# Eight plain chunks and twenty product groups instead of twelve and twelve, with attention spread into the groups

## The chip, the cores and the metric

One core of one Trainium2 chip runs the whole computation in one launch. The metric is device microseconds of one execution, as a median of several. A profile of one further execution shows what each engine did: TensorE (PE; its weight loads are PEld), VectorE (DVE), ScalarE (ACT), GpSimd (POOL), and SyncE (SP), which here only issues DMAs.

## The reference

For x of 2048 tokens by 576 features, in fp32, two branches are added to x:

```
xn  = layernorm(x)
A   = attention(xn @ wqkv) @ wo        # 32 heads of 18; each token sees 8 tokens: itself and 2, 4, ... 14 back
h   = gelu(xn @ w1), its four quarters shifted by +1, -1, +2, -2 tokens
x1  = x + h @ w2
B   = x1 + gelu(layernorm(x1) @ w3) @ w4   # w3: 576 x 4608, w4: 4608 x 576
out = x + A + B
```

## The kernel before

**Precision.** All products are taken in a split form: each fp32 operand is written as a high part, which is its cast for TensorE, and a low part, the rest. ScalarE makes the high part, VectorE subtracts it for the low part (`split_w`, `split_ws`, `split_op`, `low_part`). A product of two operands then takes three matmuls.

**Stages in order.** The qkv projection writes q, k and v to a DRAM buffer `qkvd`. The token mixer gives x1 in `Y` (16 tiles of 128 tokens) and its layernorm, transposed, in DRAM (`xn`) and on chip (`x1n`). Then comes the wide MLP, which the change is about, and at the end the product of the attention result with `wo`.

**The wide MLP.** The 4608 hidden features are 36 slices of 128, taken in pairs. The first `NPL` = 12 pairs are *plain chunks*: for each chunk and each of four blocks of 512 tokens (a *unit*, 48 in all) two `up` products give the hidden values, a gelu follows, and four `down` tiles of 128 tokens add hidden @ w4 to the result. The downs of a unit are run after the ups of the next one. The other `NWP` = 6 pairs are done by a seven-product scheme on 2 x 2 blocks (two halves of the features, two blocks of 512 tokens, two slices): a *group* `q` forms seven products P1 to P7 of seven matmuls each from sums and differences of the operands, and runs the eight down tiles D0 to D7 of the group before. A pair takes two groups, one for each half `sb` of the tokens, so there are 12 groups. The sums of x1n are made in DRAM (`sums`), loaded by `get_op` and split by `split_op` (keys B11, B21, B22, T1 to T4); those of w3 are loaded by `load_pair`, formed by `combine` on VectorE and split by `split_a` and `split_s`.

**The order around the change.** Everything is emitted by hand, and each engine runs its list in that order. In a group the string `ORDER` (or an entry of `ORDERS`) gives the sequence of P's and D's on TensorE, and `at(item, f)` puts further work behind an item in the lists of the other engines. Four PSUM buffers of one bank serve the products; P1, P6, P7 and P4 accumulate onto one of them, and before each of P6, P7 and P4 ScalarE must have copied the state (`keep`, L1063). VectorE's `z_add` (L1066) adds the other products. Two PSUM buffers serve the downs in turn.

**Evicting a down tile.** For the six tiles not in `YD` VectorE adds PSUM to `Y` (L827). For the ten in `YD` ScalarE copies PSUM to a staging tile (L823) and GpSimd issues a DMA that adds it to DRAM (`yd`, L824). In the plain stage the staging is three of the `YD` slots of `Y` (9, 11, 10), in the groups a pool `evp` of five tiles. Other `YD` slots hold scratch: the raw w4 of `load_w4`, and Z1 to Z4.

**Attention in the background.** `attention` is a generator that emits VectorE operations for eight sets of four heads, and yields an estimate of the time of each. `bg(us)` adds to a debt and emits operations while the debt is positive. In plain units from u = 4 on the debt grows by `RATE[0]` = 9.0 us a unit. `yield None` marks the point before the exp on ScalarE; the generator goes on from it only in a call with `late` true. What is left three units before the end of the plain stage is emitted at once. Before a group reads attention's result, `load_o` loads it from DRAM (`od`), and `o_turn` transposes it on VectorE; this begins in the group with `z == -5`, group 7 before and group 15 after.

Of the kernel before, what the change touches and what calls it, by code (L numbers as in the profile page):

```python
# [8 lines left out]
F32 = mybir.dt.float32  # L9
# [8 lines left out]
NT = S // 128  # L18
# [18 lines left out]
NPL = 12  # L37
# [20 lines left out]
def fused_block(ctx, tc, x, wqkv, wo, w1, w2, w3, w4, out):  # L58
# [42 lines left out]
    bncnt = [0]  # L101
    ztail = {}
# [455 lines left out]
    def split_w4(c, step=None):  # L558
        t = W4["pair", c]
        raw = Y[:, 0:4, :].rearrange("p (a b) c -> p a b c", b=2)[:, :, 1, :]  # L560
        if step != 1:
            act.copy(t[:, :, 0, :], raw)  # L562
        if step != 0:
            dve.tensor_tensor(t[:, :, 1, :], raw, t[:, :, 0, :].bitcast(F32), op=ALU.subtract)  # L564
# [107 lines left out]
    def attention(ap):  # L672
        mask = ap.tile([128, TPP, W], F32, name="mask")
        pool.memset(mask, 0.0)
        for w in range(1, W):
            pool.memset(mask[0:1, 0:DIL * w, w:w + 1], -1e9)
# [14 lines left out]
        def av(g):  # L691
# [8 lines left out]
            o = ap.tile([128, TPP * GH, HD], F32, name="o")  # L700
            for w in range(W):
                r0 = halo - DIL * w
                vv = v[:, r0:r0 + TPP, :].rearrange("p j (h d) -> p (j h) d", d=HD)
                dst = o if w == 0 else ap.tile([128, TPP * GH, HD], F32, name="prod")
# [6 lines left out]
            sp.dma_start(od.rearrange("(p j) d -> p j d", p=128)[:, :, g * GC:(g + 1) * GC],  # L711
                         o.rearrange("p (j h) d -> p j (h d)", h=GH))
# [5 lines left out]
        for g in range(NG + 1):  # L718
            if g < NG:
# [3 lines left out]
                for w in range(W):  # L723
                    prod = ap.tile([128, TPP * GH, HD], F32, name="prod")
                    r0 = halo - DIL * w
                    dve.tensor_tensor(prod.rearrange("p (j h) d -> p j (h d)", h=GH), q,  # L726
                                      k[:, r0:r0 + TPP, :], op=ALU.mult)
                    yield 1.3
                    dve.tensor_reduce(Lf[:, :, w], prod, axis=AX.X, op=ALU.add)  # L729
                    yield 1.3  # L730
# [62 lines left out]
    def low_part(h, g):  # L793
        dve.tensor_tensor(h[:, 1, :], g, h[:, 0, :].bitcast(F32), op=ALU.subtract)  # L794
# [12 lines left out]
    def down(t, parts, pd):  # L807
# [17 lines left out]
        else:  # L825
            yv = Y[:, t, :].rearrange("p (h c) -> p h c", h=2)
# [44 lines left out]
    def split_op(sb, k):  # L871
        xt = area[sb][k]
# [16 lines left out]
    def load_pair(q):  # L889
        c0 = 2 * (NPL + pair(q)) * 128  # L890
        odd = (q - (q > NWP)) % 2
        st = WS["st", q] = (evp if odd else wspool).tile([128, 3, 4, 128], F32, name="w3st")
# [4 lines left out]
        for a in range(0, 96, 32):  # L897
# [3 lines left out]
    def combine(q):  # L901
        st = WS["st", q]
        for o, i, op in ((1, 0, ALU.subtract), (0, 2, ALU.add), (2, 1, ALU.subtract),
                         (3, 2, ALU.subtract)):
            dve.tensor_tensor(st[:, 1:3, o, :], st[:, 1:3, o, :], st[:, 1:3, i, :], op=op)
            dve.tensor_tensor(st[0:96, 0, o, :], st[0:96, 0, o, :], st[0:96, 0, i, :], op=op)


    def split_ws(dst, src, steps):
# [4 lines left out]
        if 2 in steps:  # L914
            dve.tensor_tensor(dst[:, 1:3], src[:, 1:3], dst[:, 3:5].bitcast(F32), op=ALU.subtract)
# [22 lines left out]
    RATE = [9.0, 2.0]  # L938
# [6 lines left out]
    for u, (c, b) in enumerate(units):  # L945
# [8 lines left out]
        for i in range(C):  # L954
# [18 lines left out]
            if z == -1:  # L973
                split_op(0, ("T2", "T1")[i])
        if u == 1:
            raw = x1n[3].bitcast(F32)
            pool.tensor_tensor(RS[2][:, 0, 0:1], raw[:, 4, 0:1], raw[:, 8, 0:1], op=ALU.mult)
        for j, (t, parts) in enumerate(prev):
            bg(r, j == 1)
# [8 lines left out]
            for f in {(-3, 1): (lambda: split_a(0),), (-3, 3): (lambda: combine(0),),  # L988
                      (-2, 1): (lambda: split_op(0, "T3"),), (-2, 3): (lambda: split_op(0, "T4"),),
                      (-1, 0): (lambda: split_s(0, (0, 1)),), (-1, 1): (lambda: split_s(0, (2,)),),  # L990
                      (-1, 3): (lambda: split_op(0, "B22"), lambda: split_a(1))}.get((z, j), ()):
# [13 lines left out]
        if z == -3:  # L1005
            while not state["done"]:
                bg(1e9)
            apc.__exit__(None, None, None)


            opc = tc.tile_pool(name="op", bufs=1, reuse_waits="tile")
            opool = opc.__enter__()
            evc_pool = tc.tile_pool(name="evp", bufs=1, reuse_waits="tile")
# [340 lines left out]
```

## Time and profile before

| | |
|---|---|
| median of 3 runs | 1289.2 us (1289.15 to 1290.45) |
| profiled execution | 1290.47 us, its span 1288.7 us |
| TensorE busy | 1272.9 us, 99% of the span |
| VectorE busy | 920.9 us, 71% |
| ScalarE busy | 558.3 us, 43% |
| granted TensorE clock | 0.999 |
| plain units | from 313 to 925 us of the span |
| product groups | from 925 to about 1211 us |

Matmuls are pipelined, so their durations overlap, and a time per matmul is best read as the distance of two starts. Shares of the other engines are means over stages with different loads. Where a row shows idle time, it is that of the engine just before the row, with what ended it.

### The profile page before, as it was taken

The numbers are of one execution on the slowest core, as the hardware profiler recorded it, in microseconds if no ns is written. First come the engines' busy times: TensorE is split into PE (matmuls) and PEld (weight loads), VectorE is DVE, ScalarE is ACT, GpSimd is POOL, SyncE is SP. The second block draws the span as 40 slices with busy tenths as digits, with TensorE's granted clock in tenths as the row PEclk, the third lists the DMA queues.
The fourth block names the chain that finished last, engine by engine and source line by source line (L and its number), as shares of the span: only waits on it lengthen the run. The fifth ranks groups of instructions, "written<-read, shape, count | busy, mean of one in ns | idle before, by whom it ended". The sixth has DMA issues, their size and how long they took to land. (4 is left out here: it accounts for less than half of the span.)

```text
span 1288.7 us, 19585 instructions
## 1 busy us (share of the span) xinstructions
PE 1272.9 (99%) x7594; PEld 1169.8 (91%) x7594; DVE 920.9 (71%) x1307; ACT 558.3 (43%) x900; POOL 214.2 (17%) x318
## 2 busy tenths in 40 slices
PE   9999999999999999999999999999999999999998
PEld 8999998899898989899999999988898898999998
DVE  6455534677568899999999999966766656676541
ACT  3322126516634434343434343433856567455530
POOL 2011100021221211221212121112111112112200
PEclk9999999999999999999999999999999999999999
DMA  7646874246896887987876877558847777788972
GB/s 209 158 115 138 171 176 142 75 123 182 197 269 146 166 165 195 193 167 150 176 155 145 184 134 158 90 113 188 193 80 137 150 167 163 169 209 180 265 251 83
DMA packets 196172, 210.21 MB, mean 163 GB/s; under 512 B 77920, under 2 KB 134176, under 8 KB 195952
## 3 DMA queue, kind: packets, MB, share of 16 engines
q1 hardware_dynamic: 165536, 144.82, 38.9%
q0 software_dynamic: 30544, 64.16, 32.2%
q8 instruction: 59, 0.97, 0.3%
q14 instruction: 33, 0.27, 0.1%
HBM read 112.98 MB, written 107.28 MB: 171 GB/s over the span
## 5 line engine op out<-in xcount | busy, mean ns | idle before, releaser
L819 PEld LDWEIGHTS ps<-w,c 128*128 128x128 f32 x3456 | 466.7, 188 | 14.3 <-DVE Y L827 4.2
L819 PE MATMUL ps<-w,c 128*128 128x288 f32 x3456 | 473.3, 294 | 5.3 <-DVE Y L827 2.9
L824 POOL DMA_DIRECT2D yd<-Y x125 | 109.2, 876 | 445.8 <-ACT Y L823 413.2
L823 ACT COPY Y<-ps 128x576 f32<-128x576 f32 x125 | 79.9, 640 | 162.6 <-PE ps L819 84.4
L794 DVE TENSOR_TENSOR c<-Y,c 128x512 fp32r<-128x512 f32 x144 | 98.9, 687 | 59.2 <-ACT Y L784 50.5
L783 ACT ACTIVATE c<-p 128x512 fp32r<-128x512 f32 x96 | 57.6, 600 | 191.9 <-PE p L800 191.9
L212 PE MATMUL ps<-WQ,xt 128*128 128x432 f32 x672 | 134.8, 360 | 0.0
L212 PEld LDWEIGHTS ps<-WQ,xt 128*128 128x128 f32 x672 | 125.6, 188 | 5.7
L726 DVE TENSOR_TENSOR prod<-q,k 128x1152 f32<-128x1152 f32 x64 | 86.6, 1353 | 10.4 <-DMA k<-qkvd 9.7
L827 DVE TENSOR_TENSOR Y<-ps,Y 128x576 f32<-128x576 f32 x108 | 81.2, 752 | 16.0 <-PE ps L819 15.8
L729 DVE TENSOR_REDUCE L<-prod 128x64 f32<-128x1152 f32 x64 | 86.5, 1351 | 1.1
L824 POOL DMA_DIRECT2D yd<-ev x55 | 47.8, 887 | 217.6 <-ACT ev L823 214.2
L800 PE MATMUL p<-xt,w3a 128*128 128x512 f32 x336 | 78.9, 391 | 1.5 <-ACT Y L784 1.5
L800 PE MATMUL p<-x1n,w3a 128*128 128x512 f32 x336 | 78.6, 390 | 0.0
L800 PE MATMUL p<-xt,w3s 128*128 128x512 f32 x336 | 78.5, 390 | 0.0
L800 PE MATMUL p<-x1n,w3s 128*128 128x512 f32 x336 | 78.5, 390 | 0.0
L705 DVE TENSOR_TENSOR prod<-v,L 128x1152 f32<-128x1152 f32 x56 | 75.8, 1353 | 0.8
L709 DVE TENSOR_TENSOR o<-o,prod 128x1152 f32<-128x1152 f32 x56 | 75.8, 1353 | 0.6
L800 PEld LDWEIGHTS p<-xt,w3a 128*128 128x128 f32 x336 | 62.2, 188 | 15.0 <-ACT Y L784 2.3
L119 POOL TENSOR_TENSOR rs<-rs,mhalf 128x1 f32<-128x1 f32 x48 | 30.9, 645 | 261.0 <-DVE rs L118 148.0
L800 PEld LDWEIGHTS p<-x1n,w3a 128*128 128x128 f32 x336 | 62.4, 188 | 12.6
L800 PEld LDWEIGHTS p<-xt,w3s 128*128 128x128 f32 x336 | 62.4, 188 | 12.6
(196 smaller groups left out, 1759.3 us busy)
## 6 DMA issues: line engine op xcount, KB each, us to landing
yd<-Y POOLq DMA_DIRECT2D x127, 288.0 KB, 5.4
yd<-ev POOLq DMA_DIRECT2D x55, 288.0 KB, 5.1
Y<-in_B_w_dram SPq DMA_DIRECT2D x23, 576.0 KB, 6.8
w3st<-in_B_w_dram SPq DMA_DIRECT2D x44, 256.0 KB, 6.1
qkvd<-stg SPq DMA_DIRECT2D x24, 432.0 KB, 3.5
xd<-st SPq DMA_DIRECT2D x16, 320.0 KB, 6.1
xd<-big SPq DMA_DIRECT2D x16, 320.0 KB, 7.8
xin<-in_A_x_dram SPq DMA_DIRECT2D x16, 288.0 KB, 3.8
```

Of the source, the lines that this page charges most:

```text
L212: pe.matmul(ps[:, h, :n], xs(a), ws(b, h), start=i == 0, stop=i == len(PAIRS) - 1)
L705: dve.tensor_tensor(dst, vv, Lf[:, :, w:w + 1].to_broadcast([128, TPP * GH, HD]), op=ALU.mult)
L709: dve.tensor_tensor(o, o, dst, op=ALU.add)
L726: dve.tensor_tensor(prod.rearrange("p (j h) d -> p j (h d)", h=GH), q, k[:, r0:r0 + TPP, :], op=ALU.mult)
L729: dve.tensor_reduce(Lf[:, :, w], prod, axis=AX.X, op=ALU.add)
L783: act.activation(by_token(h[:, 0, :]), in_order(ps), AF.Gelu_apprx_tanh)
L794: dve.tensor_tensor(h[:, 1, :], g, h[:, 0, :].bitcast(F32), op=ALU.subtract)
L800: pe.matmul(ps, W3[f][:, w, :], x1n[b][:, a, :], start=n == 0, stop=n == len(PAIRS) - 1)
L819: pe.matmul(ps[:, k, :HF], h[:, col], w[:, p, k * HF:(k + 1) * HF], start=n == 0, stop=n == len(seq) - 1)
L823: act.copy(e.rearrange("p (h c) -> p h c", h=2), ps[:, :, :HF])
L824: pool.dma_start(yd[t], e, accum_op=ALU.add)
L827: dve.tensor_tensor(yv, ps[:, :, :HF], yv, op=ALU.add)
```

## The change

`NPL` goes from 12 to 8: 32 plain units and 20 groups. Attention no longer ends with the plain stage. The rate is 9.4 instead of 9.0, and in groups 0 to 14 `bg` is called after each item with 1.5 us less the VectorE time spent there, which the helpers now count in `spent`; its debt is capped at 4.0 instead of 2.0. The pools of attention stay open until group 15 starts, so the five staging tiles, the two tiles `place(0)` and `place(1)`, and the second staging buffer of `load_pair` are not there before: staging goes on in three slots of `Y`, T4 and B22 of both halves use a ring block, and each `load_pair` uses the one buffer in `wspool`.

In attention the window order is reversed, so that a larger w lies later in k and v; of the eight q by k windows six are taken two at a time (2304 elements an operation), and one tile `po` holds both the scratch and the result. `combine` works on 128 partitions of three slots at once, four operations instead of eight. `ORDER` alternates products and down tiles, and the steps of `at` move: `split_w4` of a middle group from D6 and D7 to D2 and P4, `load_pair` from D2 to D6, `split_a` from P2 and P6 to D0 and P5, `split_s` to P3 and D5. The `split_op`s of T4 and B22 move from the last plain units into group 0, and for the second half into groups 9 and 10.

The core of the diff, cut:

```diff
-NPL = 12
+NPL = 8
 NWP = NF // 2 - NPL
...
+        po = ap.tile([128, 2, TPP * GC], F32, name="po")
+        o = po[:, 0, :].rearrange("p (x d) -> p x d", d=HD)
+        prod = po[:, 1, :].rearrange("p (x d) -> p x d", d=HD)
...
-                for w in range(W):
-                    prod = ap.tile([128, TPP * GH, HD], F32, name="prod")
-                    r0 = halo - DIL * w
-                    dve.tensor_tensor(prod.rearrange("p (j h) d -> p j (h d)", h=GH), q,
-                                      k[:, r0:r0 + TPP, :], op=ALU.mult)
-                    yield 1.3
-                    dve.tensor_reduce(Lf[:, :, w], prod, axis=AX.X, op=ALU.add)
-                    yield 1.3
+                for w, n in ((0, 1), (1, 1), (2, 2), (4, 2), (6, 2)):
+                    dst = po[:, 2 - n:2, :]
+                    win = bass.AP(tensor=k.tensor, offset=k.offset + DIL * w * GC,
+                                  ap=[list(k.ap[0]), [DIL * GC, n], [1, TPP * GC]])
+                    dve.tensor_tensor(dst, qf[:, None, :].to_broadcast([128, n, TPP * GC]), win,
+                                      op=ALU.mult)
+                    yield 0.15 + 1.2 * n
+                    dve.tensor_reduce(Lw[:, w:w + n, :],
+                                      dst.rearrange("p w (x d) -> p w x d", d=HD),
+                                      axis=AX.X, op=ALU.add)
+                    yield 0.15 + 1.2 * n
...
-        state["debt"] = min(state["debt"] + us, 2.0)
+        state["debt"] = min(state["debt"] + us, 4.0)
...
-        odd = (q - (q > NWP)) % 2
-        st = WS["st", q] = (evp if odd else wspool).tile([128, 3, 4, 128], F32, name="w3st")
+        st = WS["st", q] = wspool.tile([128, 3, 4, 128], F32, name="w3st")
...
-            dve.tensor_tensor(st[:, 1:3, o, :], st[:, 1:3, o, :], st[:, 1:3, i, :], op=op)
-            dve.tensor_tensor(st[0:96, 0, o, :], st[0:96, 0, o, :], st[0:96, 0, i, :], op=op)
+            dve.tensor_tensor(st[:, :, o, :], st[:, :, o, :], st[:, :, i, :], op=op)
...
-    RATE = [9.0, 2.0]
+    RATE = [9.4, 2.0]
...
-    ORDER = "P1 P2 P6 P5 P7 D0 P4 D1 P3 D2 D3 D4 D5 D6 D7"
+    ORDER = "P1 P2 P6 D0 P5 D1 P7 D2 P4 D3 P3 D4 D5 D6 D7"
...
         elif z < -1:
-            at("P2", split_a, n, (0, 1))
-            at("P6", split_a, n, (2,))
             at("P1", load_w4, p)
-            at("D1" if q == 1 else "D0", combine, n)
...
+            at("D0", split_a, n, (0, 1))
+            at("P5", split_a, n, (2,))
+            at("D1", combine, n)
+            at("D2", split_w4, p, 0)
+            at("P4", split_w4, p, 1)
             at("D3", gelu22)
...
+            at("P3", low22)
+            at("P3", split_s, n, (0, 1))
+            at("D4", gelu12)
+            at("D5", split_s, n, (2,))
             at("D6", low12)
-            at("D6", split_w4, p, 0)
-            at("D7", split_w4, p, 1)
             if z < -2:
-                at("D2", load_pair, q + 2 + (q == NWP - 2))
+                at("D6", load_pair, q + 2 + (q == NWP - 2))
...
             for f in plan.get(it, ()):
                 f()
+            if z < -5:
+                bg(1.5 - spent[0], it in ("P6", "D1", "P4", "D6"))
+                spent[0] = 0.0
```

More of the change, by code (lines that the diff above doesn't have):

```diff
@@ L101, in fused_block @@
     bncnt = [0]
+    spent = [0.0]
     ztail = {}
@@ L974, in fused_block @@
                 split_op(0, ("T2", "T1")[i])
+            if (z, i) == (-1, 1):
+                x1 = ring_block(("w", 1))
+                for sb in range(2):
+                    area[sb].update(T4=x1[:, 0:5, :], B22=x1[:, 5:10, :])
+                get_op(0, "B22")
+                get_op(0, "T4")
         if u == 1:
@@ L988, in fused_block @@
             for f in {(-3, 1): (lambda: split_a(0),), (-3, 3): (lambda: combine(0),),
[L989 removed]
+                      (-2, 1): (lambda: split_op(0, "T3"),),
                       (-1, 0): (lambda: split_s(0, (0, 1)),), (-1, 1): (lambda: split_s(0, (2,)),),
[L991 removed]
+                      (-1, 2): (lambda: load_pair(1),)}.get((z, j), ()):
                 f()
@@ L1017, in fused_block @@
                 area[sb].update(B11=x2[:, 0:5, :], B21=x2[:, 5:10, :], T3=x3[:, 0:5, :])
-            area[0].update(T4=place(0), B22=place(1))
-            for k in ("B11", "B21", "T3", "T4"):
+            for k in ("B11", "B21", "T3"):
                 get_op(0, k)
```

96 lines of the change are left out of this document (47 added, 49 removed).

## The prediction

> **What bounds the kernel now.** I read the page's header first, then each engine by stretch, then TensorE in order of time, then what ended TensorE's pauses.
>
> ```profile
> span 1288.7 us, 19585 instructions
> ...
> PE 1272.9 (99%) x7594; PEld 1169.8 (91%) x7594; DVE 920.9 (71%) x1307; ACT 558.3 (43%) x900; POOL 214.2 (17%) x318
> ```
>
> ```profile
> 347.00:880.00 533.00, 531.01 (x3162) 482.99 (x3162) 479.63 (x480) 207.47 (x329) 111.94 (x139) 1.00 0.77 162
> 946.10:970.20 24.10, 24.10 (x147) 22.01 (x146) 13.76 (x23) 12.82 (x22) 4.32 (x5) 1.00 0.47 62
> ```
>
> The reader is to see that TensorE (PE) is the bound, 99% of the span, and that VectorE (DVE) hides two different stages behind it. The second pair of rows is the view by windows, with span, PE, weight load, DVE and ACT in that order: in the plain stage with attention beside it DVE works 479.63 of 533 us, 90%; in a group of seven products without attention it works 13.76 of 24.1 us, 57%. So there is room in the groups, and the change fills it.
>
> ```profile
> 361.20 6.55 PE L800 MATMUL p<-xt,w3s 128*128 128x512 f32 x28
> 367.58 6.50 PE L819 MATMUL ps<-w,c 128*128 128x288 f32 x48
> 373.92 6.55 PE L800 MATMUL p<-xt,w3s 128*128 128x512 f32 x28
> ...
> 1091.06 3.40 PE L1057 MATMUL cc<-x1n,w3a 128*128 128x512 f32 x14
> ...
> 1115.08 3.40 PE L1057 MATMUL cc<-x1n,w3a 128*128 128x512 f32 x14
> ```
>
> In TensorE's timeline one plain unit (28 up matmuls, 48 down matmuls) repeats after 373.92 - 361.20 = 12.72 us, and one undisturbed group (49 product matmuls, 96 down matmuls) after 1115.08 - 1091.06 = 24.02 us.
>
> **The change, term by term.** *TensorE's work.* Four chunks of four units go, 16 x 12.72 = 203.5 us. Eight groups come, 8 x 24.02 = 192.2 us. That is -11.4 us, as certain as the two periods, for the matmuls' shapes are unchanged; putting products and downs alternately moves them and adds none.
>
> *Pauses that go.*
>
> ```profile
> L819 PE MATMUL ps<-w,c 128*128 128x288 f32 x3456 | 473.3, 294 | 5.3 <-DVE Y L827 2.9 <-ACT Y L823 2.0 <-ACT ev L823 0.4
> ...
> L1057 PE MATMUL cc<-xt,w3s 128*128 128x512 f32 (+1 forms) x210 | 52.0, 394 | 2.6 <-ACT Y L1063 2.6
> ```
>
> The last column is TensorE's idle time and what ended it. The 2.6 us before products are two waits for `keep` in the old groups 2 and 3, where a `split_op` of T4 or B22 stands in front of it on ScalarE (ACT); after the change no group from 1 to 8 has such a `split_op`. Of the 2.9 us that a VectorE eviction ended, 2.7 lie in the plain stage and at the end of attention there (0.2 at the very end stay). They come from D0 or D2 tiles whose PSUM buffer is wanted again soon, and in the built program's order buffers of plain D0 tiles that are wanted again three tiles later fall from 17 to 7, since there are fewer units. With the 0.4 us of `ev` I take -5.7 us; the bounds are 0 (other pauses in their place) and -5.7.
>
> *VectorE in the groups.*
>
> ```profile
> L794 DVE TENSOR_TENSOR c<-Y,c 128x512 fp32r<-128x512 f32 x44 | 30.2, 687 | 12.7 <-ACT Y L790 7.7 <-ACT Y L784 4.4
> L827 DVE TENSOR_TENSOR Y<-ps,Y 128x576 f32<-128x576 f32 x32 | 24.2, 755 | 13.0 <-PE ps L819 12.9
> L1066 DVE TENSOR_TENSOR Y<-cc,Y 128x512 f32<-128x512 f32 x33 | 22.8, 691 | 50.7 <-ACT Y L1063 30.9 <-PE cc L1057 19.7
> L905 DVE TENSOR_TENSOR w3st<-w3st 128x256 f32<-128x256 f32 x40 | 16.6, 415 | 0.1
> L564 DVE TENSOR_TENSOR w<-Y,w 128x1152 fp32r<-128x1152 f32 x10 | 13.6, 1358 | 2.6 <-ACT w L562 2.2
> L915 DVE TENSOR_TENSOR w3s<-w3st,w3s 128x1024 fp32r<-128x1024 f32 x10 | 12.1, 1205 | 0.8 <-ACT w3s L911 0.8
> ...
> L589 DVE SCALAR_TENSOR_TENSOR xt<-xt 128x1024 fp32r<-128x1024 f32 x4 | 4.9, 1224 | 9.5 <-ACT xt L876 9.5
> ```
>
> An attention operation of 1152 elements costs what L564 does, 1.36 us. From 512 to 1152 elements the slope is (1.358 - 0.687) / 640 = 1.05 ns, so a new double window of 2304 is estimated at 1.358 + 1.21 = 2.57 us, between nothing saved (2.72) and no fixed part (2.4). One head group then has 19 single and 6 double operations and some 4 us of short ones, 45 us, and eight have 361 us. The plain stage takes 26 units x 9.4 = 244 us and a little, which leaves 110 us for 13 to 14 groups, 8 us each. With 13.8 us of their own, less 0.6 for `combine` in four pieces instead of eight, the groups stand at 21 of 24 us, 88%. VectorE does not become the bound, but its order does matter.
>
> I number a group's fifteen places at 1.6 us: P1 0, P2 1.6, P6 3.2, D0 4.8, P5 6.4, D1 8.0, P7 9.6, D2 11.2, P4 12.8, D3 14.4, P3 16.0, D4 17.6, D5 19.2, D6 20.8, D7 22.4, end 24.0. With two PSUM buffers D6 needs D4's. In new group 2 a double reduction stands in VectorE's order between P3's work and D4's eviction: P3 ends at 17.6, z_add 18.3, low part 19.0, reduction 21.5, eviction 22.3, and D6 was due at 20.8: +1.5 us. Elsewhere only single operations stand there, worth 0 to 0.2.
>
> *ScalarE, exp among the groups.*
>
> ```profile
> L823 ACT COPY ev<-ps 128x576 f32<-128x576 f32 x52 | 33.1, 636 | 59.9 <-PE ps L819 59.9
> L789 ACT ACTIVATE c<-Y 128x512 fp32r<-128x512 f32 x33 | 20.9, 634 | 1.9 <-DVE Y L1066 1.9
> L790 ACT ACTIVATE Y<-Y 128x512 f32<-128x512 f32 x33 | 20.9, 632 | 1.0
> L1063 ACT COPY Y<-cc 128x512 f32<-128x512 f32 x34 | 20.0, 590 | 32.2 <-PE cc L1057 30.5 <-ACT w3a L913 1.7
> L562 ACT CAST w<-Y 128x1152 fp32r<-128x1152 f32 x10 | 11.6, 1155 | 0.0
> ```
>
> ```profile
> 561.72 1.28 ACT L742 ACT_TABLE_LOAD   x1
> 563.01 0.63 ACT L742 ACTIVATE L<-L 128x512 f32<-128x512 f32 x1
> ```
>
> Two of the eight exps fall into groups. In group 3 it stands after D6's eviction: that ends at 23.0, table 24.3, exp 24.9, D7's eviction 25.5, the table back 26.8, two gelus 28.0, `keep` 28.6, which is 4.6 in group 4, where P6 is due at 3.2: +1.3 us. [...] The other exp is in group 9, behind P6, with that group's five `split_op`s: `keep` of P7 comes at 10.5 with P4 due at 9.6 (its order has P4 earlier), then two attention operations and a `split_op` (1.22 + 0.69) before D2's eviction: 0.9 + 0.6 + 0.6 = +2.1 us.
>
> *Groups 0 and 1.* Group 0 has eleven places, 17.6 us, and now also T4, B22 and the next `split_a`. VectorE's list is z_add, B22 1.9, D0, two single operations, z_add, low part, split 1.5, T4 1.9, and T4 is ready at about 15.5 for P4 due at 14.4 (+1.1). The split of S then ends 0.6 late for group 1's P6. `load_pair(2)` waits for it because only one staging buffer is left, lands at 12 in group 1, the casts hold `keep`, and P4 is 1.4 late. Together +3.1 us, bounds 0 and 6.
>
> *The end of attention.*
>
> ```profile
> 1067.09 7.78 SPq L1092 DMA_DIRECT2D Y<-od  x12
> 1074.98 0.40 SPq L555 DMA_DIRECT2D Y<-in_B_w_dram  x1
> ...
> 1106.68 1.51 SPq L895 DMA_DIRECT2D w3st<-in_B_w_dram  x2
> 1108.24 1.41 SPq L898 DMA_DIRECT2D w3st<-in_B_w_dram  x3
> ```
>
> ```profile
> Y<-in_B_w_dram SPq DMA_DIRECT2D x23, 576.0 KB, 6.8
> w3st<-in_B_w_dram SPq DMA_DIRECT2D x44, 256.0 KB, 6.1
> ...
> od<-o SPq DMA_DIRECT2D x8, 576.0 KB, 7.6
> ```
>
> SP's queue in the built program is: `load_pair(16)` (six issues), the last store of `od`, twelve `load_o` that read `od`, and then group 15's `load_w4`. Before, `od` had long landed when group 7 read it. Now the pair starts when S is split, 23.2 in group 14, takes 1.51 + 4 x 0.47 = 3.4, the store is issued at 26.6 and lands at 34.2, which is 10.2 in group 15. The twelve loads take 7.8, and w4 lands 6.8 later, at 24.8. But `split_w4`'s cast has moved from D6 to D2, so it waits at the head of ScalarE from 11.8 on, and behind it are D3's eviction, gelu22 and gelu12. D3 is evicted after 1.16 + 0.64, at 26.6, and D5, due at 19.2, waits 7.4; with VectorE's half of the split in front of D4's eviction another 1.4. That is 8.8 by medians; the lower end is 0, if all three transfers together end 9 us sooner. I take +7.0, nearer the upper working, since the medians are from busier stretches.
>
> *Sum.* -11.4 - 5.7 + 1.5 + 1.3 + 2.1 + 3.1 + 7.0 = -2.1 us. The profiled execution took 1290.47 us for its span of 1288.7, 1.27 above the median of 1289.2; so 1288.4 for such an execution, and 1287.1 us for a median. A measurement of this kernel tells about 0.2%, 2.6 us, from no change, so the forecast lies at the edge of it.
>
> **The rivals.** *Waits stay hidden* (faster). All new waits but 4 us vanish because transfers land early and operations overlap: 1289.2 - 17.1 + 4, with 3 us of old pauses back, 1279 us. For it speaks that 44 units at 90% VectorE had only 2.7 us of such pauses; against it the SP order above.
>
> *The single staging buffer* (slower). Every group's `load_pair` is issued only after D5's split, 23.2, and its last transfer starts at 26.2 and lands 6.1 later, 8.3 in the next group. Casts end 1.4 after that, then gelu c11 1.27, D1's eviction 0.64, `keep` 0.59, and P4 is due at 12.8: it decides from a landing at 8.9, 0.6 us later than the median gives. Each further us holds P4 by one us. At 0.8 us in 13 groups, 10 us: 1297 us.
>
> *VectorE falls behind* (slower). Double windows of 2.57 us at 88 to 90% load put evictions late in plain units and groups alike, say 0.25 us in each of 26 units and 14 groups: +10 less 3 already counted, 1294 us.
>
> **How the numbers follow.** Forecast 0.45, its own range 1283 to 1291 (faster 0.19, within 0.2% 0.22, slower 0.04); hidden waits 0.27; single buffer 0.20; VectorE behind 0.08. So faster 0.46, same 0.22, slower 0.32. For 8 in 10 the range reaches through most of the first rival and to the second: 1277 to 1297.
>
> **What would show it.** Periods of 12.72 and 24.02 us in undisturbed units and groups. Pauses before D6 of group 2, P6 of group 4, P4 of groups 0 and 1, in group 9, and above all before D5 of group 15, ended by an ACT eviction behind a cast that waits for w4's DMA. No pause in group 15 makes the forecast too slow; P4 pauses in most groups make it too fast; a double window far from 2.57 us upsets VectorE's share.

## The result, and the profile after

The changed kernel takes 1301.1 us as a median of six runs (1298.58 to 1305.05), the kernel before 1289.62 (1288.58 to 1291.67): a ratio of 1.0088, with a 95% interval of 1.0069 to 1.0106. It is 0.9% slower, where the prediction had 1287.1 us. The profiled run of the changed kernel is the fastest of the six, 1298.58 us with a span of 1296.8; its lines below belong to that one.

The head of its page, then two stretches in the view by windows (span, PE, weight load, DVE, ACT, POOL, then the granted clock): the plain stage and group 13.

```profile
span 1296.8 us, 19623 instructions
...
PE 1268.3 (98%) x7538; PEld 1164.3 (90%) x7538; DVE 971.4 (75%) x1299; ACT 596.3 (46%) x952; POOL 214.4 (17%) x318
```

```profile
347.00:694.00 347.00, 343.85 (x2051) 312.70 (x2049) 314.37 (x283) 137.32 (x216) 78.38 (x93) 1.00 0.85 188
1045.56:1069.66 24.10, 24.10 (x148) 21.99 (x147) 21.23 (x27) 13.10 (x21) 4.38 (x6) 1.00 0.59 119
```

TensorE's busy time fell by 1272.9 - 1268.3 = 4.6 us only, not by the 11.4 us of removed work, and its idle time in the span rose from 15.8 to 28.5 us. VectorE is busy 21.23 us in a group of 24.1, as the prediction had it (21).

TensorE's timeline, with the pause before a row in brackets and what ended it. These are the longer pauses of the last plain units, groups 0 to 10 and group 15:

```profile
708.26 3.23 PE L828 MATMUL ps<-w,c 128*128 128x288 f32 x12 [2.56 <-ACT Y L832]
...
723.62 1.86 PE L828 MATMUL ps<-w,c 128*128 128x288 f32 x12 [0.81 <-DVE Y L837]
...
750.17 3.35 PE L1059 MATMUL cc<-xt,w3s 128*128 128x512 f32 x7 [3.29 <-ACT Y L1065]
753.33 3.00 PE L828 MATMUL ps<-w,c 128*128 128x288 f32 x12
756.16 1.78 PE L1059 MATMUL cc<-xt,w3s 128*128 128x512 f32 x7
757.78 1.75 PE L828 MATMUL ps<-w,c 128*128 128x288 f32 x12
...
796.13 3.44 PE L828 MATMUL ps<-w,c 128*128 128x288 f32 x24 [1.33 <-DVE Y L837]
...
828.10 1.88 PE L1059 MATMUL cc<-xt,w3s 128*128 128x512 f32 x7 [1.26 <-ACT Y L1065]
...
956.33 1.89 PE L1059 MATMUL cc<-xt,w3a 128*128 128x512 f32 x7 [0.90 <-ACT Y L1065]
...
974.47 1.85 PE L828 MATMUL ps<-w,c 128*128 128x288 f32 x12 [0.94 <-ACT Y L832]
...
1111.78 1.87 PE L1059 MATMUL cc<-xt,w3s 128*128 128x512 f32 x7 [1.85 <-DVE Y L1069]
...
1117.02 2.52 PE L828 MATMUL ps<-w,c 128*128 128x288 f32 x12 [1.78 <-ACT ev L832]
```

The reader is to see two things. The pauses stand at named places, not spread over the units. And behind the longest ones the matmuls themselves are slow: twelve down matmuls take 3.00 us at 753.33 and 1.75 at 757.78. The view by windows of that stretch, PE alone with the granted clock after its busy time, shows why:

```profile
748.40:749.20 0.80, 0.00 (x0) 1.00 0.03 10
749.20:750.00 0.80, 0.00 (x0) 0.54 0.20 33
750.00:750.80 0.80, 0.63 (x2) 0.50 0.86 264
...
755.60:756.40 0.80, 0.80 (x6) 0.69 0.49 173
756.40:757.20 0.80, 0.80 (x5) 1.00 0.02 6
```

The granted clock is halved from 749.2 to about 756.1 us, and likewise for about 3.4 us from 708.3 and from 1117.9. Summed as (1 - clock) times time, the three stretches come to 1.71, 3.41 and 1.71 us, 6.83 in all, beside a missing busy time of 11.4 - 4.6 = 6.8. This sum is an upper bound of what they cost, for TensorE itself was idle for 0.90 and 0.20 us inside the last two.

### The profile page after: what moved, and what is told of

Its sections match the earlier page's. It is cut to its first block, busy times and chain, and to the rows that moved or that the text cites. A ratio compares the mean times of both kernels' runs of the same rounds, so it can differ in the third digit from the quotient of the medians.

```text
span 1296.8 us, 19623 instructions
## 1 busy us (share of the span) xinstructions
PE 1268.3 (98%) x7538; PEld 1164.3 (90%) x7538; DVE 971.4 (75%) x1299; ACT 596.3 (46%) x952; POOL 214.4 (17%) x318
## 4 chain that ended last, share of the span: by engine, by line
PE 61%; issue 19%; DVE 7%; DMA 6%; POOL 3%; ACT 3%; SPq 1%; POOLq 0%; DVEq 0%; ACTq 0%
PE ps L828 18%; PE ps L213 16%; PE p L809 9%; PE cc L1059 9%; PE ps L463 4%; POOL yd L833 3%; PE ps L310 3%; DMA yd<-Y 2%; DVE L L735 1%; DMA xt<-td1T 1%; DVE po L732 1%; DVE c L803 1%; PE ps L478 1%; ACT Y L832 1%; DVE Y L837 1%
## 5 line engine op out<-in xcount | busy, mean ns | idle before, releaser
L832 ACT COPY Y<-ps 128x576 f32<-128x576 f32 x157 | 100.2, 639 | 191.6 <-PE ps L828 136.4
L1059 PE MATMUL cc<-xt,w3s 128*128 128x512 f32 x420 | 108.4, 398 | 6.4 <-ACT Y L1065 4.5
L837 DVE TENSOR_TENSOR Y<-ps,Y 128x576 f32<-128x576 f32 x108 | 81.3, 753 | 25.0 <-PE ps L828 24.8
L1059 PEld LDWEIGHTS cc<-xt,w3s 128*128 128x128 f32 x420 | 77.7, 190 | 22.4 <-ACT Y L1065 5.4
L732 DVE TENSOR_TENSOR po<-q,k 128x2304 f32<-128x2304 f32 (+1 forms) x40 | 82.9, 2074 | 16.0 <-issue 10.9
L708 DVE TENSOR_TENSOR po<-v,L 128x1152 f32<-128x1152 f32 x64 | 86.2, 1354 | 0.9
L735 DVE TENSOR_REDUCE L<-po 128x128 f32<-128x2304 f32 (+1 forms) x40 | 82.7, 2068 | 0.2
L712 DVE TENSOR_TENSOR po<-po 128x1152 f32<-128x1152 f32 x56 | 75.7, 1353 | 0.6
L1069 DVE TENSOR_TENSOR Y<-cc,Y 128x512 f32<-128x512 f32 x60 | 41.3, 689 | 39.5 <-PE cc L1059 27.9
L1059 PE MATMUL cc<-x1n,w3a 128*128 128x512 f32 (+1 forms) x280 | 67.9, 393 | 0.0
L1065 ACT COPY Y<-cc 128x512 f32<-128x512 f32 x60 | 35.2, 586 | 67.2 <-PE cc L1059 64.5
L1059 PEld LDWEIGHTS cc<-x1n,w3a 128*128 128x128 f32 (+1 forms) x280 | 51.6, 188 | 10.3
L213 PE MATMUL ps<-W,h 128*128 128x288 f32 x384 | 53.5, 295 | 0.0
```

The source lines that it names most:

```text
L213: pe.matmul(ps[:, h, :n], xs(a), ws(b, h), start=i == 0, stop=i == len(PAIRS) - 1)
L732: dve.tensor_tensor(dst, qf[:, None, :].to_broadcast([128, n, TPP * GC]), win, op=ALU.mult)
L735: dve.tensor_reduce(Lw[:, w:w + n, :], dst.rearrange("p w (x d) -> p w x d", d=HD), axis=AX.X, op=ALU.add)
L832: act.copy(e.rearrange("p (h c) -> p h c", h=2), ps[:, :, :HF])
L837: dve.tensor_tensor(yv, ps[:, :, :HF], yv, op=ALU.add)
L1059: pe.matmul(ps, WX[w][:k, v, SLOT[w], :], area[sb][xk][:k, a, :], start=onto is None and i == 0, stop=last and i == len(HALVES) - 1, skip_ ...
```

## The experiments

Line numbers shift by 2 to 12 between kernels. The kernel before took 1288.7 to 1290.2 us beside these runs. The half-clock stretches of a run are called stretches.

**Planted pauses.** On the kernel before, in fourteen places of the plain stage:

```diff
+            if (u, i) in HOLD:
+                for n in HOLD[u, i]:
+                    act.copy(RT[:, :n], RT[:, :n])
+                w = W3[c * C + i][:, PAIRS[0][1], :]
+                act.copy(w, w.bitcast(F32))
             up(u, c, b, i)
```

> The kernel before, with fourteen planted pauses of TensorE in the plain stage: ahead of an up tile ScalarE copies scratch data (0 to 4 copies of 0.4 to 0.63 us) and then the tile's first weights onto themselves, so that TensorE waits about 1.0 to 3.6 us; twice two such waits stand 4 us apart. Theory A (the clock halves after a long pause): pauses below about 2 us show clock 1.00 after them, those above some bound between 1.33 and 2.56 us show 0.50 for 3 to 7 us, and the time rises by the planned pauses, some 29 us, and 1.5 to 2.8 us for each long one. Rival (the half clock at 708, 749 and 1118 us has other reasons, such as busy DMA or what VectorE does): no 0.50 after planted pauses, the time rises by their length alone.

One run: 1328.85 us, clock 0.995. The planted pauses came out at 0.97 to 4.12 us, and four stretches followed, each of 1.71 us. Against the profile of the kernel before, TensorE's idle time rose by 30.1 us and its busy time, for the same matmuls, by 8.3 (1281.2 - 1272.9), of which the stretches are 6.8; so the length of the pauses alone is not the price. TensorE's timeline, the pause in brackets:

```profile
495.09 8.25 PE L800 MATMUL p<-x1n,w3s 128*128 128x512 f32 x28 [4.12 <-ACT w3s L964]
...
577.19 8.26 PE L800 MATMUL p<-xt,w3s 128*128 128x512 f32 x28 [1.93 <-ACT w3s L964]
619.38 6.65 PE L800 MATMUL p<-x1n,w3s 128*128 128x512 f32 x28 [2.14 <-ACT w3s L964]
660.40 6.64 PE L800 MATMUL p<-x1n,w3a 128*128 128x512 f32 x28 [2.58 <-ACT w3a L964]
...
743.30 6.65 PE L800 MATMUL p<-xt,w3a 128*128 128x512 f32 x28 [3.23 <-ACT w3a L964]
785.46 8.24 PE L800 MATMUL p<-x1n,w3a 128*128 128x512 f32 x28 [3.72 <-ACT w3a L964]
```

The 28 matmuls after a pause take 8.25 us with a stretch and 6.65 without. A pause of 1.93 us brought one, a pause of 3.23 us none, so length alone does not decide. The stretches began at 495.72, 577.64, 785.86 and 874.60 us (windows of 0.02 us). In the trace of the changed kernel a single stretch lasts 3.413 us (half of it lost, 1.71), and the later starts here lie 24.0, 85.0 and 111.0 such lengths after the first; in the changed kernel they lie at 708.30, 749.26 and 1117.90, the later two 12.0 and 120.0 lengths after the first. Such lengths, laid end to end both ways from the first stretch of a run, held 1.88 to 3.02 us of TensorE's idle time just ahead of the four stretches here, and 1.78 to 2.56 just ahead of the three in the changed kernel; the fullest of the others held 1.82 here (of the 3.23 us pause, 1.41 and 1.82 fell into two lengths) and 1.33 there. With the rate alone changed (below) one that held 1.83 had no stretch behind it, so these counts overlap by 0.05 us. The stretch from 749.26 in the changed kernel is two lengths, with 0.90 us of idle time in the first and none in the second; that of 3.41 us from 1117.9 has 0.20. The count tells the 1.93 us from the 3.23 us here; by what rule the clock is granted is not shown. Theory A holds, but not its bound of about 2 us: pauses of 1.88 and 1.93 us brought a stretch, and four of 2.14 to 3.23 us none.

**Group 15's loads.** w4's load first, and then the last `od` store also ahead of `load_pair(16)`:

```diff
         if z == -5:
+            load_w4(p)
             while not state["done"]:
...
+            if (z, it) == (-6, "D5"):            # second kernel only
+                while not state["done"]:
+                    bg(1e9)
```

> Changed kernel (median 1301.1 us), with group 15's load_w4 issued ahead of the last od store and the twelve load_o. Theory A (two separate waits in group 15, and a clock that halves after them): the wait of the w4 cast goes, 1.78 + 0.20 us, and with it the half-clock stretch of 1.6 us behind it; the 1.85 us pause stays, since VectorE's o_turn waits for load_o in front of a z_add: 1297.5 us. Theory B (the prediction's: the w4 cast is the whole loss of group 15): 1.85 + 1.78 + 0.20 + 1.6 go, 1295.7 us. Theory C (only the length of a pause counts): 1299.1 us.

> As the kernel with w4 first, and the last attention operations and their od store go out at D5 of group 14, ahead of load_pair(16) on SP's queue (the store started at 1096.69 us behind six loads that began at 1093.03). Theory A: the store lands some 5 us earlier, o_turn finds its tile, both pauses of group 15 go (1.85 + 1.78 + 0.20) and no half-clock stretch is left there: 1301.1 - 5.4 = 1295.7 us. Rival: load_o's transfers are late for another reason (twelve loads at 5.7 us on one queue), the 1.85 us pause stays: 1297.5 us.

Measured: 1294.23 us (1293.29 to 1299.44, ratio 1.0045, 1.0029 to 1.0061) and 1293.64 us (1291.13 to 1297.48, ratio 1.0036, 1.0020 to 1.0052). In the profile of the first the 1.78 us pause and the stretch at 1117 us are gone and 1.41 of the 1.85 us pause stays; in the second one pause of 0.92 us is left there. What was queued, in the timelines of SP's queue, VectorE and ScalarE of the changed kernel:

```profile
1093.03 1.01 SPq L905 DMA_DIRECT2D w3st<-in_B_w_dram  x2
...
1096.69 0.52 SPq L714 DMA_DIRECT2D od<-po  x1
1104.79 5.70 SPq L1094 DMA_DIRECT2D Y<-od  x12
...
1110.24 0.71 DVE L159 STREAM_TRANSPOSE big<-Y 128x512 f32<-128x512 f32 x1 [5.35 <-DMA Y<-od]
...
1110.53 0.42 SPq L556 DMA_DIRECT2D Y<-in_B_w_dram  x1
...
1115.27 1.15 ACT L563 CAST w<-Y 128x1152 fp32r<-128x1152 f32 x1 [9.53 <-DMA Y<-in_B_w_dram]
```

That is the predicted chain, pair, store, twelve loads, w4, cast, and beside it one that was not predicted: VectorE waits for `load_o` in `o_turn` and holds a z_add behind it. As theory A had it, these are two waits. The medians fell by 6.9 and 7.5 us, where 3.6 and 5.4 were expected: the waits are shown, the surplus is not explained by them. In both profiles the pause of group 1 brought 1.71 us of stretches instead of 3.41, and the changed kernel's own median moved by 3 us between two sets of runs (below). By the median alone theory B's 1295.7 us for the first kernel would fit as well; it is the remaining pause in the profile that decides for A.

**Attention held at the change of stages.**

```diff
-    RATE = [9.4, 2.0]
+    RATE = [9.4, 0.0]
...
-                bg(1.5 - spent[0], it in ("P6", "D1", "P4", "D6"))
+                if q > 1:
+                    bg(1.6 - spent[0], it in ("P6", "D1", "P4", "D6"))
```

> Changed kernel with no attention operation in the last two plain units and in groups 0 and 1 (16 us of VectorE work), made up by 1.6 us instead of 1.5 an item from group 2 on. Theory A (VectorE's crowding by attention at the change of stages): the pauses of 2.56 and 0.81 us in the last plain units and of 3.29 and 0.23 in groups 0 and 1 go, with half-clock stretches of 1.5 and 2.8 us: -11.2 us, less 0 to 3 for fuller later groups: 1290 to 1293 us, clock 0.998. Rival (the pauses there come from the stage's own work: split_op of T4 and B22, combine, split of S, one staging buffer): 1298 to 1301 us.

1309.29 us (1304.6 to 1312.32, ratio 1.0150, 1.0130 to 1.0170), above both ranges. My theory fell: the pauses of 2.56 and 3.29 us stood to 0.01 us, only the 0.81 went, and the 0.23 became 0.52. And a new one came; TensorE's, SP's and VectorE's timelines of this run:

```profile
708.01 2.90 PE L828 MATMUL ps<-w,c 128*128 128x288 f32 x12 [2.57 <-ACT Y L832]
...
749.94 3.20 PE L1059 MATMUL cc<-xt,w3s 128*128 128x512 f32 x7 [3.29 <-ACT Y L1065]
...
1024.44 6.71 SPq L689 DMA_DIRECT2D v<-qkvd  x1
1036.92 2.63 DVE L708 TENSOR_TENSOR po<-v,L 128x1152 f32<-128x1152 f32 x2 [11.50 <-DMA v<-qkvd]
1040.27 3.25 PE L828 MATMUL ps<-w,c 128*128 128x288 f32 x12 [8.48 <-DVE Y L837]
```

The budget made up in the later groups put the first use of the last v right behind its load, and VectorE stood 11.50 us at it. The hold in units -2 and -1 also came too late: operations that the program puts into the unit before them run on VectorE when TensorE is already in the next (in the changed kernel `combine` of unit -3 starts at 701.59 us, and TensorE has begun unit -2 at 694.39).

**The 2.56 us pause.** ScalarE's and VectorE's timelines of the changed kernel ahead of 708.26 us:

```profile
700.32 1.36 DVE L708 TENSOR_TENSOR po<-v,L 128x1152 f32<-128x1152 f32 x1
701.59 2.33 DVE L916 TENSOR_TENSOR w3st<-w3st 128x384 f32<-128x384 f32 x4
704.44 1.22 DVE L591 SCALAR_TENSOR_TENSOR x1n<-x1n 128x1024 fp32r<-128x1024 f32 x1
705.69 0.68 DVE L591 SCALAR_TENSOR_TENSOR x1n<-x1n,Y 32x512 fp32r<-32x512 f32 x1
706.40 0.63 ACT L888 ACTIVATE Y<-x1n 32x512 fp32r<-32x512 f32 x1 [3.34 <-DVE x1n L591]
707.59 0.62 ACT L832 COPY Y<-ps 128x576 f32<-128x576 f32 x1
```

The second `split_op` writes the scratch row `RT` (L888) that the first one's VectorE half (L591) still has to read; that half stands behind attention and `combine`, and the eviction L832 behind L888. A scratch tile of its own, on the kernel with `od` and w4 first:

```diff
-        r = RT.bitcast(F32R)
+        r = (temp(13) if sb == 0 and k in ("B21", "T1") else RT).bitcast(F32R)
```

> From the kernel with od and w4 first: the split_op of B21 and T1 use a second scratch tile instead of the one that B11 and T2 use. Theory A (the 2.57 us pause before the fourth down tile of the last plain unit but one: ScalarE stands 3.34 us in front of that tile's eviction, waiting for VectorE to release the shared scratch, and VectorE is behind with attention that was issued a unit earlier): the pause goes, with a half-clock stretch: 1293.6 - 2.57 - 1.71 = 1289.4 us. Rival (VectorE's backlog holds TensorE by its own evictions instead): the pause stays or only changes its releaser, 1292 to 1294 us.

1290.3 us (1287.01 to 1295.83, ratio 1.0010, 0.9995 to 1.0024). L888 now runs at 702.67 and the four down tiles of that unit in one piece (TensorE's and ScalarE's timelines of this run):

```profile
700.36 6.50 PE L828 MATMUL ps<-w,c 128*128 128x288 f32 x48
...
703.86 0.62 ACT L832 COPY Y<-ps 128x576 f32<-128x576 f32 x1
```

The pause is gone, and the stretch behind it; the median is 3.3 us lower, 4.3 were expected. The cause of this pause is shown.

**Group 0's list, load_xa, and all three**, each on the kernel with `od` and w4 first:

```diff
+        if z == -1:
+            split_w4(NPL)
...
-            at("D1", split_op, 0, "T4")
-            at("D2", combine, n)
+            at("P6", split_op, 0, "T4")
+            at("D1", combine, n)
             at("D2", low22)
-            at("D2", split_w4, p)
```

> From the kernel with od and w4 first (median 1293.64 us): in group 0 the split_op of T4 goes from D1 to P6 and combine from D2 to D1, and group 0's split_w4 goes ahead of the last plain unit. Theory A (the 3.26 us pause at P6 of group 1 is the end of a serial list: T4's split, combine, half of split_w4 and the split of S stand one behind the other on VectorE and ScalarE in eleven places): the pause falls below 1 us, the 0.54 us pause before P4 of group 0 goes, and with them one or two half-clock stretches of 1.71 us: 1293.6 - 3.3 - 0.5 - 1.7 = 1288 us. Rival (the single staging buffer: load_pair's late landing holds group 0 whatever the order): the pause stays above 2.5 us, 1292 to 1294 us.

```diff
+    XA = [t for t in range(NT) if t not in YD] + list(YD)
...
-        if 13 <= u < 13 + NT:
-            load_xa(u - 13)
         if 14 <= u < 14 + NT:
-            add_x(u - 14)
+            load_xa(XA[u - 14])
+        if 15 <= u < 15 + NT:
+            add_x(XA[u - 15])
```

> From the kernel with od and w4 first: the ten accumulating DMAs of load_xa into yd start at unit 20 and the six plain loads go to units 14 to 19, so that the former no longer run beside the accumulating DMAs of sums (units 5 to 20). Theory A (load_xa moved from unit 21 to 13 collides with sums on Pool's queue; ScalarE's copies into the three staging tiles then wait up to 7 us for yd): the pauses near 500 and 555 us (0.43 and 3.14 in the profiled run, with a half-clock stretch of 1.71) go: 1293.6 - 2 to 5 = 1289 to 1291.5 us, and the runs spread less than now (6 us). Rival (the staging waits come from the attention's own loads of q, k and v at these places): pauses stay, 1293 to 1294 us.

> The three edits together on the kernel with od and w4 first. If the three causes are separate, the gains add: 1293.6 - 5.5 - 3.5 - 4.3 = 1280 us, clock 0.999, below the kernel before (1289.6 us). Rival (they share VectorE's backlog, so that one pause goes and the next takes its place): 1286 to 1289 us.

Group 0's list. In the changed kernel the casts of S waited 2.73 us on ScalarE for `combine` (L916), and the `keep` (L1065) that P6 of group 1 needs stood behind them (ScalarE's timeline):

```profile
744.42 1.06 ACT L921 CAST w3s<-w3st 128x1024 fp32r<-128x1024 f32 x1 [2.73 <-DVE w3st L916]
...
749.52 0.60 ACT L1065 COPY Y<-cc 128x512 f32<-128x512 f32 x1
```

With the edit the pause before P6 of group 1 fell from 3.26 to 1.29 us (below 1 was expected), and the 0.54 and the stretch at 754 us went, as expected; but the median stayed, 1294.94 us (ratio 1.0042, 1.0027 to 1.0056). In its profile the last v came due behind its load again: VectorE stood 9.51 us at it, and TensorE paused 6.49 us at 1032, with 3.41 us of stretches, in part while it still waited. That the time saved let attention run ahead is the likely reason, not a shown one.

load_xa: 1294.15 us (1289.43 to 1298.38, ratio 1.0034, 1.0023 to 1.0046). The profiled run, one of the fastest of its twelve, has 0.27 us near 500 and no pause near 555 us. But the kernel with w4 first alone has neither in its profile, without this edit, and the kernel with all three edits has both again (1.04 and 1.55), so the theory that load_xa makes them is not borne out.

All three: 1297.6 us (ratio 1.0063, 1.0047 to 1.0078), above both ranges and slower than any one, for two reasons in its profile: the v load again (a pause of 6.69 us) and w4's cast, which I had put ahead of the last unit, where w4 was not yet there (ScalarE's and TensorE's timelines):

```profile
713.68 1.16 ACT L563 CAST w<-Y 128x1152 fp32r<-128x1152 f32 x1 [5.06 <-DMA Y<-in_B_w_dram]
...
723.33 3.25 PE L828 MATMUL ps<-w,c 128*128 128x288 f32 x12 [4.25 <-ACT Y L832]
```

**Group 0 mended otherwise, and the rate.** On the kernel with the second scratch: `split_w4` of group 0 at P1, T4 at P6, `combine` at D1, and a wait in the budget before the last v is used. Three variants of it follow.

```diff
+                    if g == NG - 1:
+                        yield 8.0
...
-            bg(r, j % 2 == 1)                    # second and fourth kernel
+            bg(r, j == 1)
...
-    RATE = [9.4, 2.0]                            # third and fourth kernel
+    RATE = [9.0, 2.0]
-                bg(1.5 - spent[0], ...
+                bg(1.6 - spent[0], ...
```

> From the kernel with the second scratch (median 1290.3 us): in group 0 split_op of T4 at P6, combine at D1, split_w4 at P1 (not ahead of the last plain unit, where ScalarE's cast stood 5.06 us waiting for w4's DMA), and attention waits 8 us of its budget between the load of the last v and its first use (VectorE stood 9.7 to 11.5 us for that load in two runs). Theory A (each pause has its own serial list in front of it): the pause before P6 of group 1 falls from 3.28 to about 1.3 us as it did, its half-clock stretch goes, the 0.53 us before P4 goes, no pause near 1035 us: 1290.3 - 2.0 - 0.5 - 1.7 = 1286 us. Rival (whatever is taken from one list comes back in the next, as with the three edits together, 1297.6): 1290 to 1294 us.

> As the kernel with group 0 mended, and in the plain stage an exp may go out only behind the second down tile of a unit, as in the kernel before, not also behind the fourth. Theory A (the pauses near 555 us come from exp, which waits 4.1 to 5.2 us on ScalarE for VectorE's subtraction while a down tile's eviction stands behind it; in the fourth place that eviction is wanted at once): fewer pauses near 500 to 555 us and less spread: 1 to 2 us faster, 1284 to 1285 us. Rival (VectorE is as late in either place): same within 1 us.

> As the kernel with group 0 mended, with attention at 9.0 instead of 9.4 us a plain unit (the rate of the kernel before) and 1.6 instead of 1.5 us an item in the groups. Theory A (VectorE's backlog in the plain stage, 96% busy there, makes its evictions and exp late): pauses at 332, 397, 500 and 555 us shrink, and the spread of the runs too: 1 to 3 us faster, 1283 to 1285 us. Rival (the plain pauses are waits for yd and q, k, v transfers at fixed places; fuller groups show new pauses): same or 1 to 3 us slower.

> Both: exp only behind the second down tile, and 9.0 and 1.6 us. If the two act on the same backlog, their gains overlap: 1283 to 1285 us. If the groups cannot take more attention, 1287 us or more.

Measured: 1293.07 us (ratio 1.0028, 1.0016 to 1.0039), 1297.74 (1.0072, 1.0060 to 1.0084), 1284.77 (0.9968, 0.9957 to 0.9979) and 1285.14 (0.9963, 0.9949 to 0.9977). In the first two the pause of group 1 is 1.29 and 1.30 us, as expected, but the wait for v shifted attention so far that what was left went out at once at D5 of group 14, six and thirteen operations of 1.36 us in a row; TensorE paused 2.79 and 12.54 us there. With exp behind the second down tile only, TensorE has no pause from 410 to 700 us in the second kernel's profile, but 1.93 us at 604 in the fourth's. So my own added wait put the second kernel far above its range, and the first into that of its rival (1290 to 1294); the last two came out as expected. Their gain has two parts that these runs do not separate: no such lump any more, since 9.0 and 1.6 us finish attention earlier, and less backlog in the plain stage. Where exp may go out made no difference that can be told at 9.0 us.

**The rate alone**, on the changed kernel: 9.0 and 1.6, nothing else.

> The changed kernel (median 1301.1 us) with only two numbers changed: attention at 9.0 instead of 9.4 us a plain unit, 1.6 instead of 1.5 us an item in the groups. Theory A (VectorE's backlog at the end of the plain stage stands behind most of the loss, and attention that ends earlier in group 14 stores od earlier): the pauses of 2.57 and 0.81 us in the last plain units, 1.85 and 1.78 in group 15 and the plain ones near 500 and 555 us go with two half-clock stretches; the 3.29 us in group 1 stays: 1290 to 1292 us. Theory B (single serial lists, the rate matters little): 1298 to 1302 us.

1295.24 us (1291.68 to 1299.95, ratio 1.0046, 1.0027 to 1.0065). That is 3 to 6 us below the changed kernel's two medians, and between the two theories: the plain pauses near 500 and 555 us are not in its profile (nor in that of w4 first, at 9.4) and the 2.56 us pause is 1.81, without a stretch; the 3.27 us of group 1 stays, and group 15 pauses 3.51 us before one down tile. There the store of `od` was long done, and the twelve loads alone (6.52 us of issuing) held w4's load back.

**The changed kernel again.**

> The changed kernel as it is, a second profile. If the pauses belong to the order written in the program: the same places (708, 724, 750, 796, 828, 956, 974, 1112, 1117 us) within 0.1 us each, with only the plain pauses (332 to 555 us) and the number of half-clock stretches differing: 1298 to 1305 us, median 1301. If they are chance: other places.

1297.97 us (1295.48 to 1303.0, ratio 1.0074, 1.0054 to 1.0093); the profiled run took 1302.19. The pauses repeat: 2.56, 0.80, 3.29, 1.33, 1.26, 0.89 and 0.93 us at the same places of the program, 3.2 to 3.5 us later in the span, and 2.02 and 2.13 in group 15 (two transfers). The 3.6 us between the profiles are mostly the plain stage and the clock: 3.13 us instead of 1.07 near 553 us, and five stretches of 1.71 us instead of four. ScalarE and VectorE ahead of that pause:

```profile
544.54 0.64 ACT L832 COPY Y<-ps 128x576 f32<-128x576 f32 x1 [6.76 <-DMA yd<-Y]
547.80 0.64 ACT L832 COPY Y<-ps 128x576 f32<-128x576 f32 x1 [2.62 <-DMA yd<-Y]
...
549.46 0.69 DVE L803 TENSOR_TENSOR c<-Y,c 128x512 fp32r<-128x512 f32 x1 [5.49 <-ACT Y L792]
550.07 2.55 DVE L735 TENSOR_REDUCE L<-po 128x128 f32<-128x2304 f32 x1
```

ScalarE waits for a staging slot (`yd` not yet landed), gelu comes late, VectorE idles 5.49 us and is then late itself, at a rate that leaves it little slack (in the changed kernel's first profile it is busy for 191.31 of the 200 us from 450 us on). How long the slot is late differs from run to run; why the transfer is late there stays open.

**Single windows**, on the kernel of 1284.77 us: `for w, n in [(w, 1) for w in range(W)]`.

> From the kernel with group 0 mended and 9.0 and 1.6 us (median 1284.77 us): all windows single, as in the kernel before. 48 operations of 1.35 us take the place of 24 of 2.55 and 48 more in all of QK: VectorE works some 3.6 us more (24 pairs x 0.15). If long operations put evictions late (the prediction's third rival): the pauses at 602 us (1.43) and in group 2 (3.34 with a stretch of 3.41) shrink: 1279 to 1283 us. If it is VectorE's total alone: 1 to 4 us slower, 1286 to 1289 us.

1284.04 us (1282.86 to 1284.81, ratio 0.9958, 0.9945 to 0.9971). VectorE is busy 975.1 instead of 970.5 us, the pauses at 602 us and in group 2 and the stretches are gone, others came. The median is between the two ranges. The test is not a clean one: in group 2 this kernel issues w4's load at 766.02 us, ahead of a store of `od` and of the loads of v, and its cast does not wait; with double windows the load stands behind them (below). So what went there cannot be put down to the length of the operations, and on balance the double windows neither cost nor save.

**w4's load behind D4 of the group before**, on the kernel of 1284.77 us:

```diff
...
+        if q < NQ - 6 and q != NWP - 1:
+            at("P4" if q == 0 else "D4", raw_w4, NPL + pair(q + 1))
```

> From the kernel with group 0 mended and 9.0 and 1.6 us: w4's load for the next group is issued behind D4 of the group before, ahead of load_pair on SP's queue, instead of at P1. Theory A (the 3.34 us pause before D6 of group 2: ScalarE's cast of w4 waits 5.46 us for the load, VectorE's half of the split, then a double product, z_add and D4's eviction come behind it): the pause falls to 1.3 us or less, without a half-clock stretch of 1.71 or 3.41: 1284.8 - 4 = 1281 us. Theory B (the double operation itself holds D4's eviction): the pause stays above 2 us, 1284 to 1286 us.

1280.96 us (1279.54 to 1281.86, ratio 0.9930, 0.9915 to 0.9944), clock 1.000. In the kernel without it, w4's load in group 2 stood in SP's queue behind the load of v. Its cast ended its wait at 781.64, and the rest came behind it (the timelines of SP's queue, ScalarE, VectorE and TensorE):

```profile
767.43 5.91 SPq L689 DMA_DIRECT2D v<-qkvd  x1
...
773.87 0.43 SPq L556 DMA_DIRECT2D Y<-in_B_w_dram  x1
...
781.64 1.16 ACT L563 CAST w<-Y 128x1152 fp32r<-128x1152 f32 x1 [5.46 <-DMA Y<-in_B_w_dram]
782.83 1.36 DVE L566 TENSOR_TENSOR w<-Y,w 128x1152 fp32r<-128x1152 f32 x1 [4.37 <-ACT w L563]
784.11 2.55 DVE L732 TENSOR_TENSOR po<-q,k 128x2304 f32<-128x2304 f32 x1
...
788.58 5.99 PE L830 MATMUL ps<-w,c 128*128 128x288 f32 x24 [3.34 <-DVE Y L839]
```

With it that pause is gone, no stretch stands before the last matmul, and TensorE is busy 1262.0 us, 10.9 less than before the change. This version is faster than both kernels: 8.3 us below the kernel before, and 17 to 20 below the changed one.

## Why the prediction was wrong

By its own steps, against the profiled run of the changed kernel (the sum of spans is +8.1 us):

| step | predicted | in the profile |
|---|---|---|
| TensorE's work | -11.4 | -11.4: periods 488.31 - 475.59 = 12.72 and 1069.64 - 1045.60 = 24.04 |
| old pauses go | -5.7 | -3.4: 2.6 before `keep` went; the plain stage kept 4.2 of 4.9 |
| last two plain units | 0 | +5.1: 2.56 + 0.81 + 1.71 of stretch |
| groups 0 and 1 | +3.1 | +6.4: 0.23 + 3.29, and 2.8 in slow matmuls |
| group 2 before D6 | +1.5 | +1.33 |
| exp, P6 of group 4 | +1.3 | +1.26 |
| groups 9 and 10 | +2.1 | +2.30: 0.90 + 0.46 + 0.94 |
| group 15 | +7.0 | +5.4: 1.85 + 1.78 + 0.20 and 1.6 in slow matmuls |
| start of the kernel and rest | 0 | +1.1 |

**What held.** The periods, VectorE's 21 us a group, the double window (2.55 us, 2.57 estimated), and the waits before D6 of group 2, P6 of group 4 and P4 of group 9, each in its place, behind the chain foreseen and nearly in its size (1.33, 1.26 and 0.90 us; 1.5, 1.3 and 0.9 predicted). The rest of group 9's row agrees by luck: its 0.46 and 0.94 us stand before D6 of group 9 and D1 of group 10, not at D2's eviction. Group 15's chain was right up to the wait; w4 landed 21.6 us into the group instead of 24.8, the twelve loads taking 5.70 us instead of 7.78 and w4 less than its median. So the wait it was priced for is 1.98 us; that the row comes to 5.4 is luck too, since 1.85 of it are the wait of `o_turn` and 1.6 the clock.

**The step that failed first** is pricing a pause by its length. The sum has no term for the clock; the three stretches make 6.1 us of the table's rows, six tenths of the difference between -2.1 and +8.1. In the trace of before the longest pause is 1.50 us, at the start of the plain stage, and 1.32 behind it, and the clock is 1.00 up to the last matmul, so that trace could not show the price.

**The second** is the change from plain units to groups, costed at nothing for the last two units and by 3.1 for groups 0 and 1. I had followed the moves of T4 and B22 and the split of S, and put P6 of group 1 late by 0.6 us; it was 3.29. The 1.1 and 1.4 us before P4 of groups 0 and 1 came out at 0.23 and nothing. What I missed in the plain units is a resource: the shared scratch `RT` couples ScalarE to VectorE, and VectorE is half a unit behind at 9.4 us (7.20 of 12.72 us at 701.59). The second scratch shows the one; the edits to group 0 show the other, down to the 1.29 us that stay.

**The third**, -5.7 for old pauses, took it that fewer tight buffers mean fewer pauses. The one that was followed, the 3.13 us of the repeated run, came from late slots of `yd` and a VectorE without slack. Whether the rate has a part in those near 500 and 555 us is not shown: at 9.4 us a unit they come and go (w4 first has none in its profile), and at 9.0 four of five profiles have at most 0.35 us there, but three of these pause 1.43 to 1.93 us near 603, and the one with single windows 1.28 at 552. VectorE's share by windows is 90% before and 91% after (314.37 of 347 us), so its load alone doesn't tell why the kernel before had none there. That stays open.

**The rivals.** *Waits stay hidden*: no. *The single staging buffer*: refuted, though its 1297 us comes nearest to the measured time; it has P4 late in most groups, and P4 pauses only in groups 0 and 9 (0.23 and 0.90 us). *VectorE falls behind*: right in kind for the plain stage, wrong in its mechanism and size for the groups; its double windows are in the wait of group 2, as in the forecast, and no run shows that they cost more. The median lies 2.5 us above the profiled run, probably by the plain stage and the number of stretches: in these the repeated run's profile differs from the first.

## What to carry to other kernels

Price a pause of the bound engine together with what its clock does behind it; here the two waits of 1.33 and 1.26 us had no half clock behind them, and the one of 2.56 us had a stretch of 1.71. When work is spread as a background, look for every scratch row, staging slot and queue that it shares with what the bound engine waits for, and order the loads on a queue by the time at which they are needed: moving w4's load alone was worth 3.8 us. A budget that is delayed comes due somewhere, and a forced finish at the end turned it into pauses of up to 12.5 us.

## What had not been expected of the hardware

The clock granted to TensorE was 0.50 behind some pauses, and from within one, and 1.00 behind others. In the changed kernel's profile it was 0.50 for 3.41 us from 708.3 (pause of 2.56 us), for 6.83 us from 749.3 (3.29 us) and for 3.41 us from 1117.9 (1.78 us): 1.71, 3.41 and 1.71 us of lost clock. Behind its pauses of 1.33 and 1.26 us in groups 2 and 4 it was 1.00. With planted pauses it was 0.50 behind 1.88, 1.93, 3.72 and 4.12 us, and 1.00 behind 2.14, 2.58, 2.79 and 3.23 us.

The same pause was not always worth the same. That of 3.26 to 3.29 us in group 1 brought 3.41 us of lost clock in both profiles of the changed kernel, where its last 0.90 and 1.22 us fell into the half clock, and 1.71 us in two edits that left it alone: with w4 first, where it ended 1.24 us before the half clock began, and with the rate alone, where its last 0.51 us fell into it.
